# Weight parts made only for the block pairs that use them, and new orders for the second pair and the steady pairs

## The chip, the cores and the metric

One core of one Trainium2 chip. The metric is the device time of one execution in microseconds (us); several runs are taken and the median is compared. The kernel computes in float32; its large products run in a float32 format that TensorE reads in one pass (f32r), each operand split into parts so that the result keeps its precision.

## The reference

A short convolution over time with softmaxed taps per head, then an RMS norm and a SwiGLU feed-forward:

```
x: (8, 4096, 192); weight: (8 heads, 7 taps); d_ff = 1536
w = softmax(weight, axis=-1)
out[b,s,h] = sum_k w[h,k] * x_padded[b, s+k, h]      # 24 channels a head
x = out.reshape(32768, 192)
xn = x / sqrt(mean(x*x) + 1e-6) * rms_g
g = xn @ w_gate;  val = xn @ w_val
return (g * sigmoid(g) * val) @ w_out
```

## The kernel before

**Tiling.** The 32,768 tokens are worked in 32 "pairs" of 2 x 512 tokens. A sequence has 4096 tokens, so every fourth pair begins a new sequence. The 1536 feed-forward columns are 12 blocks of 128, taken as 6 block pairs j = 0..5. For a pair of token halves and a pair of blocks there are four cells a, b, c, d, each holding gate (lower bank) and value (upper bank) in PSUM.

**The two matmul phases of a steady pair.** First the gate and value products: `FORM` says for each j whether the four cells come from 12 direct products (0: words A, B, E for the three thirds of d_model, with the cell's letter) or from 11 (1: words P1 to P7 and Q1 to Q4, a 2x2 scheme over sums of token halves and sums of weight blocks). That makes 3 x 12 + 3 x 11 = 69 products, each of six matmuls (three split parts, two row halves of the array). Then 42 steps o1.k to o7.k, a seven-form 2x2 scheme for the product with w_out; each is six matmuls on 32-column strips and accumulates into one of three PSUM accumulators X, Y, Z. `LINE` is the order of these 111 entries on TensorE.

**Words.** The rest of a pair's work is written as words in `ORDER`, emitted once for each w = 2..32. A word's first letter is the engine (A ScalarE/ACT, V VectorE/DVE, G GpSimd/POOL, S the SyncE DMA queue), then the act; "+" is for the pair after w, "++" two after, "-" the pair before; pN emits N entries of `LINE`. All engines run their own instructions in this order. The acts:

- `gc.j`, `mc.j`: SiLU of a cell's gate (L978) and multiplication with its value (L985); the PSUM bank is free after both. `f1`, `f3`, `f4`, `f5` hand partial sums of the 11-product scheme between banks (L669, L972).
- `h1` to `h4`: the sums of the hidden cells that the seven-form scheme needs (L955). `h2.k` overwrites the cell that form 6 reads.
- `c1`, `s7`, `c2`, `C22`, `C21`, `T11` to `T22`: copies of accumulators, final sums (L1002) and transposes (L943) into the output tile; `st` stores it (L1034). The o3 steps write into X again after C22 has read it.
- For the pair ahead: `ld` loads x (L148; at the start of a sequence `ld.0` issues three transfers instead of one, among them the zeros of L152), `cv0` to `cv6` the taps (L439, L435), `sq`, `red`, `pow`, `bc`, `mul` the norm, `pl` writes the normed tokens to DRAM (L1045), `ft` fetches them back transposed (L640; ft.0 and ft.2 are 512 KB, ft.4 and ft.5 256 KB, ft.1 and ft.3 issue nothing), `x1` to `x4` sums of token halves (L829), and `n`, `l`, `d` with a group number the three split parts (copy or cast L669/L671, subtraction L815, scaled subtraction L817). Groups 0, 1, 2 are the thirds of d_model, 3 and 4 the sums.

**Weight parts.** Ten right-hand operands (o = 0..9), for all 6 block pairs, are made once and kept in DRAM (`wd`). `prepare(o)` makes one in six stages (word `W` runs the next stage): POOL forms the difference (L751), DVE masks off the high bits (L754) and ACT scales a copy (L758), DVE subtracts (L760), POOL subtracts (L764), ACT casts (L766), SP stores (L770). Its buffer alternates between two halves, so operand o waits for the store of o - 2. Operands 2, 4, 6, 8 are used by the 11-product form alone, 9 by the direct form alone; `blocks(o)` says for which j an operand is made. In `FORM = (0, 1, 0, 1, 1, 0)` neither set is evenly spaced, so it returns all six. Steady products read the operands through a ring of ten slots (`ring_load`, L787), each slot refilled when its last product has been issued.

**Start.** Pair 0 is computed without splits. Pair 1, the second pair, runs 24 plain products (`PLAIN`, L873) and its 42 steps in the order `FIRST`, and in its shadow the weight parts are made and pair 2 is normed, placed, fetched and split; word R starts the ring.

## Time and profile before

| | us |
|---|---|
| median of 3 runs (lowest, highest) | 2511.77 (2506.93, 2516.0) |
| the profiled execution's own time | 2515.36 |
| its span, first to last instruction | 2512.7 |
| pair 0, up to the second pair's first product | 125.1 |
| second pair | 125.1 to 233.9 |
| pairs 2 to 31 | 233.9 to 2505.6 |
| after the last matmul | 2505.6 to 2512.7 |

The profile is one execution. In a row of a timeline stand start, duration, engine, source line, operation, what it writes and reads, the number of instructions merged, and in brackets the idle time before it and what ended that. In a row of waits stand the total, how often, and the longest. In a row of a group stand the count, the busy time and mean (ns) of one, and the idle time before them. PE is TensorE's matmuls, PEld its weight loads. Line numbers are those of the kernel before.

### The profile page before, as it was taken

The numbers are of one execution on the slowest core, as the hardware profiler recorded it, in microseconds if no ns is written. First come the engines' busy times: TensorE is split into PE (matmuls) and PEld (weight loads), VectorE is DVE, ScalarE is ACT, GpSimd is POOL, SyncE is SP. The second block draws the span as 40 slices with busy tenths as digits, with TensorE's granted clock in tenths as the row PEclk, the third lists the DMA queues.
The fourth block names the chain that finished last, engine by engine and source line by source line (L and its number), as shares of the span: only waits on it lengthen the run. The fifth ranks groups of instructions, "written<-read, shape, count | busy, mean of one in ns | idle before, by whom it ended". The sixth has DMA issues, their size and how long they took to land.

```text
span 2512.7 us, 69361 instructions
## 1 busy us (share of the span) xinstructions
PE 2468.5 (98%) x29332; PEld 1950.8 (78%) x29332; DVE 2031.6 (81%) x2402; ACT 955.2 (38%) x1344; POOL 1096.0 (44%) x719
## 2 busy tenths in 40 slices
...
GB/s 149 59 215 101 171 198 171 167 169 160 170 200 165 171 152 161 185 184 162 160 163 168 198 168 171 176 166 159 194 175 165 175 162 152 205 164 169 168 151 93
DMA packets 704967, 415.21 MB, mean 165 GB/s; under 512 B 508890, under 2 KB 690962, under 8 KB 704658
## 3 DMA queue, kind: packets, MB, share of 16 engines
...
q14 instruction: 78, 0.64, 0.1%
...
## 4 chain that ended last, share of the span: by engine, by line
PE 90%; DVE 3%; DMA 2%; SPq 2%; issue 1%; POOL 1%; ACT 1%; DVEq 0%; ACTq 0%; POOLq 0%
PE ps L901 56%; PE ps L928 33%; PE ps L873 1%; SPq L148 1%; DVE tt L829 1%; DMA wd<-part 1%; DVE y L439 1%; DMA ht<-in_moe_w_val_dram 0%; DMA ring<-wd 0%; SPq L232 0%; POOL part L764 0%; DVE ht L1100 0%; SPq L1034 0%; DMA hs<-in_moe_w_out_dram 0%; DVE part L760 0%
## 5 line engine op out<-in xcount | busy, mean ns | idle before, releaser
L901 PE MATMUL ps<-part,ring 64*128 64x512 f32 x12420 | 1430.2, 388 | 1.1 <-DVE tt L1002 0.5
L901 PEld LDWEIGHTS ps<-part,ring 64*128 64x128 f32 x12420 | 1196.4, 184 | 228.3 <-issue 13.2
L978 ACT ACTIVATE tt<-ps 128x512 f32<-128x512 f32 x744 | 439.1, 599 | 943.0 <-PE ps L901 859.4
L985 DVE TENSOR_TENSOR ht<-ps,tt 128x512 f32<-128x512 f32 x744 | 498.5, 686 | 292.2 <-ACT tt L978 290.4
L955 POOL TENSOR_TENSOR ht<-ht 128x512 f32<-128x512 f32 x243 | 358.2, 1479 | 459.0 <-PE ps L928 210.3
L928 PE MATMUL ps<-ht,wo_sb 128*32 128x384 f32 (+2 forms) x7272 | 458.4, 383 | 14.3 <-DVE tt L1002 13.4
L928 PEld LDWEIGHTS ps<-ht,wo_sb 128*32 128x32 f32 x7272 | 327.8, 111 | 113.3 <-DVE tt L1002 14.8
L928 PE MATMUL ps<-ht,x 128*32 128x384 f32 (+2 forms) x6696 | 413.2, 379 | 0.0
L439 DVE SCALAR_TENSOR_TENSOR y<-xh,tp,y 128x1536 f32<-128x1536 f32 x186 | 366.8, 1972 | 0.2
L928 PEld LDWEIGHTS ps<-ht,x 128*32 128x32 f32 x6696 | 294.4, 110 | 88.4
L955 POOL TENSOR_TENSOR hs<-ht 128x512 f32<-128x512 f32 x90 | 116.9, 1299 | 427.8 <-DVE ht L985 427.8
L972 DVE TENSOR_TENSOR ps<-ps,tt 128x1024 f32<-128x1024 f32 x180 | 221.9, 1233 | 42.2 <-ACT tt L669 32.9
L955 DVE TENSOR_TENSOR ht<-ht 128x512 f32<-128x512 f32 x129 | 147.0, 1140 | 63.7 <-PE ps L928 63.6
L669 ACT COPY ps<-ps 128x384 f32<-128x384 f32 (+1 forms) x121 | 104.1, 860 | 204.9 <-PE ps L928 147.5
L815 POOL TENSOR_TENSOR part<-xb,part 128x1024 fp32r<-128x1024 f32 x58 | 176.6, 3044 | 0.0
L669 ACT CAST part<-xb 128x1024 fp32r<-128x1024 f32 x87 | 88.6, 1047 | 215.3 <-DMA xb<-xd 214.3
L955 DVE TENSOR_TENSOR ht<-hs,ht 128x512 f32<-128x512 f32 x124 | 165.1, 1351 | 0.3 <-PE ps L928 0.3
L815 POOL TENSOR_TENSOR part<-tt,part 128x1024 fp32r<-128x1024 f32 x30 | 86.2, 2875 | 178.2 <-ACT part L669 178.2
L928 PE MATMUL ps<-hs,x 128*32 128x128 f32 (+2 forms) x2232 | 142.4, 383 | 6.7 <-DVE tt L671 6.7
L817 DVE SCALAR_TENSOR_TENSOR part<-part,xb 128x1024 fp32r<-128x1024 f32 x87 | 131.4, 1511 | 6.9 <-ACT part L669 6.9
L928 PEld LDWEIGHTS ps<-hs,x 128*32 128x32 f32 x2232 | 100.5, 111 | 36.7 <-DVE tt L671 7.0
L669 ACT COPY tt<-ps 128x384 f32<-128x384 f32 (+1 forms) x121 | 106.6, 881 | 21.4 <-PE ps L901 11.3
...
## 6 DMA issues: line engine op xcount, KB each, us to landing
...
xh<-in_x_dram SPq DMA_DIRECT2D x192, 105.0 KB
...
```

The costliest lines, as they stand in the source:

```text
L148: queue(eng).dma_start(out=dst, in_=src)
L439: nc.vector.scalar_tensor_tensor(out=y, in0=xk, scalar=w, in1=y, op0=ALU.mult, op1=ALU.add)
L669: nc.scalar.copy(out=dst, in_=src)
L815: e.tensor_tensor(out=split_of(g, 1).bitcast(F32R), in0=src, in1=high, op=ALU.subtract)
L817: nc.vector.scalar_tensor_tensor(out=split_of(g, 2).bitcast(F32R), in0=high, scalar=1.0 + SPLIT, in1=src, op0=ALU.mult, op1=ALU.subtract,)
L829: engine[eng].tensor_tensor(out=dst, in0=a, in1=b, op=op)
L901: nc.tensor.matmul(out=self.both(j, c)[:, h, :], lhsT=left[HALF[h]], rhs=right[HALF[h]], start=(first and q == 0), stop=True, skip_group_c ...
L928: nc.tensor.matmul(out=self.acc(b)[i * Q : (i + 1) * Q, at : at + n], lhsT=left, rhs=cols, start=fresh, stop=True, skip_group_check=True, ...
L955: engine[eng].tensor_tensor(out=dst, in0=a, in1=b, op=op)
L972: nc.vector.tensor_tensor(out=self.both(j, c), in0=self.both(j, "b"), in1=s5, op=ALU.add)
L978: nc.scalar.activation(out=tt[:, t, :], in_=self.both(j, c)[:, 0, :], func=AF.Silu)
L985: nc.vector.tensor_tensor(out=self.hv(j, "abcd".index(c)), in0=self.both(j, c)[:, 1, :], in1=tt[:, t, :], op=ALU.mult,)
```

## The change

Five things. (1) `HOME` gives each block pair a place in the weights, the three 11-product pairs first (j = 1, 3, 4 in places 0, 1, 2), and all readers of the weights go through it. (2) `blocks(o)` therefore returns three adjacent places for operands 2, 4, 6, 8 and 9, so those five are made and stored with half the columns. (3) `FIRST`, (4) `ORDER` and `LINE` are other orders of the same acts; some acts change engine. (5) Acts for pair 2 that `FIRST` has already done are remembered in `ahead_done` and are not done again when `ORDER` names them for w = 2.

```diff
+    HOME = tuple(
+        sum(FORM[:j]) if on else sum(FORM) + j - sum(FORM[:j]) for j, on in enumerate(FORM)
+    )
     ORDER = (
-        "p2- p6 Vd.3 Vcv3+ p2 Vl.3 VT12- p2 Agd.0 VT21- An.4 p2 Agc.0 Aga.0 Vmc.0 Vmd.0 Gl.4",
-        "p2 Aga.2 Vma.0 Vd.4 Vma.2 Af1.1 Vcv4+ p6 Af3.1 Agb.2 Aga.1 Vf4.1 Vmb.2 p6 Vcv5+",
...
-        "Agd.3 Agc.2 Vmd.3 Agb.3 p3 Vmc.2 Vmb.3 Af1.4 Agd.2 p2 Gh1.1 Gpow+ Vbc+ Gmul+ Af3.4",
-        "Spl.0+ Spl.1+ Vmd.2 Spl.2+ p3 Vf4.4 p1 Spl.3+ Spl.4+ Spl.5+ p4 Spl.6+ Spl.7+ Aga.4",
-        "Sst1.1- Sld.0++ Sst0.4- Vma.4 Sft.0+ Sft.1+ Sft.2+ Sst1.3- Sst0.3- Sft.4+ Vf5.4",
-        "Sft.3+ Sld.1++ Sst0.0- Agb.5 Agc.4 Sld.2++ Sst0.2- p1 Sld.3++ Sst1.2- Sld.4++",
-        "Sld.5++ Sld.6++ Sft.5+ p2 Vh1.3 Vmb.5 Agd.4 Agb.4 p3 Vmd.4 Sld.7++ Sst0.1- Sst1.0-",
-        "Vmb.4 p2 Agc.5 p4 Vh1.4 Vmc.4 Gh3.1 Gh1.2 Gh3.2 Gh3.0 Agd.5 Aga.5 Vmd.5 Vh1.5 Vma.5",
-        "p6 Gh3.4 Vh3.3 Vh2.0 Vh2.4 Vmc.5 p2 Vh2.2 Ac1 An.0+ Vd.0+ Vx3+ Vh2.3 Gh3.5 p7 An.1+",
-        "As7 Gh2.1 Gh2.5 p6 An.2+ p4 Vh4.4 Gh4.2 Gx1+ Gl.0+ Vc2 p7 Gh4.0 p2 Gh4.3 p2 Vh4.5",
-        "Vd.1+ Vh4.1 Vx2+ Vl.2+ Vd.2+ An.3+ Acv0++ Vx4+ Gl.1+ VC22 VT11 Vcv1++ VT22 p2 VC21",
-        "p2 Vcv2++",
+        "p4 Vd.2 p1 Vd.3 Vcv1+ VT12- p4 Vcv2+ p2 Vcv3+ p1 Agd.0 Aga.2 An.4 Aga.0 Gl.4 Vmd.0",
+        "Vma.2 Vma.0 p4 Sst1.4- Agc.0 Vmc.0 Vcv4+ Af1.1 p1 Af3.1 Vf4.1 p1 Vd.4 p2 Agb.2 p1",
...
+        "Vred+ Agd.3 Agc.2 Vmd.3 p1 Vmc.2 Vmc.3 p4 Agb.3 Gh1.0 Gh1.1 Gpow+ Vmb.3 Af1.4 p3",
+        "Agd.2 Vbc+ Vh3.0 Gmul+ Af3.4 Vmd.2 Spl.0+ p2 Spl.1+ Spl.2+ Spl.3+ Spl.4+ Vf4.4 p5",
+        "Sst0.0- Spl.5+ Spl.6+ Sst0.4- Aga.4 Gh1.3 Vh1.2 Vma.4 Vf5.4 Vh3.1 Spl.7+ Agb.5 Agc.4",
+        "Sld.0++ p3 Agd.4 Vh3.2 Vmb.5 Vmc.4 p1 Vmd.4 Sft.2+ Sft.0+ Sft.1+ Sst1.1- Sst1.2-",
+        "Sst0.1- Sft.3+ Sft.4+ p7 Agb.4 Agc.5 p1 Aga.5 Vmb.4 Vma.5 p4 Sft.5+ Sld.1++ p3 Vmc.5",
+        "Agd.5 Vmd.5 Vh2.0 Gh3.3 Gh1.4 Vc1 Gh3.4 An.0+ Gh1.5 Gh2.4 Gh2.3 Gh2.1 Vh3.5 Vh2.2",
+        "Vx1+ Vx2+ Vh2.5 p15 As7 Gh4.4 Ac2 p9 An.1+ An.2+ Sld.2++ Sld.3++ Sst1.0- Sst0.2-",
+        "Sld.4++ Sst0.3- Sst1.3- Sld.5++ Gh4.3 Gh4.1 Gx3+ Sld.6++ Sld.7++ Acv0++ Vh4.0 Vh4.2",
+        "Vx4+ Vn.3+ Vd.0+ Vl.0+ Vl.3+ Vh4.5 VC22 p4 Gl.2+ p6 Vd.1+ VT22 Vl.1+ VC21 p1 VT11",
+        "VT21",
     )
     FIRST = (
-        "p1 Vcv5+ W p2 Vcv6+ p1 Aga.0 Vma.0 p2 Asq+ W W p1 Agb.0 W Vmb.0 W p1 Vred+ p2 Agc.0",
...
-        "Gh2.5 p1 Vh2.2 p1 Gh2.1 Sld.3++ p1 Ac1 Vh2.3 An.0+ p2 Sld.4++ An.1+ Vd.0+ p1 Sld.5++",
-        "p1 As7 p1 Sld.6++ Vx3+ p1 Gh4.2 p2 Gx1+ p1 Sld.7++ p1 Vd.1+ Gl.0+ Gl.1+ An.2+ Vd.2+",
-        "Vl.2+ Vx2+ Vx4+ R p2 Vh4.4 p1 Gh4.0 p1 Vh4.5 p1 Vc2 p2 Vh4.1 p4 An.3+ p1 Acv0++ p2",
-        "VC22 p1 VT11 Gh4.3 p1 Vcv1++ p2 VC21 p3 Vcv2++ VT22",
+        "p1 W p3 Aga.0 Vma.0 p2 W W p1 Agb.0 W Vmb.0 W p3 Agc.0 Vmc.0 W p1 W Vcv5+ W W p1 W",
...
+        "p1 Gh2.1 p1 Vc1 Vh2.5 Vx1+ p2 Vx2+ Sld.1++ p1 Gh4.1 p1 Vh4.0 Sld.2++ p1 Vh4.2",
+        "Sld.3++ p2 Vx4+ p1 Vn.3+ p1 Vd.0+ Sld.4++ p1 Vl.0+ p2 As7 An.1+ Vd.1+ Vl.1+ An.2+",
+        "Vd.2+ Gl.2+ Gx3+ R Vl.3+ p1 Sld.5++ Gh4.4 p1 Sld.6++ p2 Ac2 Sld.7++ p2 Vh4.5 p4 VT11",
+        "Gh4.3 p3 Acv0++ VC22 p6 VC21 p4 VT22 VT21",
     )
     LINE = (
-        "Aa.0 Ad.0 Ed.0 Bd.0 Ac.0 Ec.0 Ea.0 Bc.0 Ba.0 Aa.2 Ea.2 Ba.2 Ab.2 P1.1 Bb.2 P5.1 P6.1",
...
-        "Ea.5 o1.0 o1.4 o7.0 o7.2 o1.5 o1.2 o1.1 o1.3 o7.4 o7.1 o7.5 o7.3 o6.4 o2.2 o6.2 o6.5",
-        "o6.0 o4.4 o6.1 o2.4 o2.0 o2.5 o6.3 o4.1 o2.1 o5.1 o5.3 o5.4 o5.2 o4.5 o5.5 o5.0 o2.3",
-        "o4.0 o4.2 o4.3 o3.5 o3.3 o3.1 o3.4 o3.2 o3.0",
+        "Aa.2 Ba.2 Ad.0 Aa.0 Bd.0 Ac.0 Ea.2 Ed.0 Ec.0 Ea.0 Ba.0 Bc.0 P1.1 Ab.2 P5.1 Bb.2 P6.1",
...
+        "Ed.5 o1.0 o1.4 o1.2 o1.3 o1.1 o1.5 o7.0 o7.4 o2.1 o2.0 o2.2 o7.3 o6.2 o6.0 o7.5 o6.1",
+        "o7.2 o7.1 o2.4 o6.5 o6.4 o6.3 o4.2 o2.5 o5.1 o5.0 o5.5 o2.3 o5.2 o5.3 o5.4 o4.4 o4.0",
+        "o3.2 o4.3 o4.5 o4.1 o3.4 o3.3 o3.5 o3.0 o3.1",
     )
@@ blocks
-        mine = [j for j in range(NP) if kind in (None, FORM[j])]
-        step = {b - a for a, b in zip(mine, mine[1:])}
-        if len(step) > 1:
-            return slice(0, NP)
-        return slice(mine[0], mine[-1] + 1, step.pop() if step else 1)
+        mine = sorted(HOME[j] for j in range(NP) if kind in (None, FORM[j]))
+        return slice(mine[0], mine[-1] + 1)
@@ ring_load
-        r = (j * NW + o) * P
+        r = (HOME[j] * NW + o) * P
@@ products (the plain ones)
-                                out=self.both(j, c)[:, h, :], lhsT=wf[HALF[h], k, 2 * j + f, :],
+                                out=self.both(j, c)[:, h, :], lhsT=wf[HALF[h], k, 2 * HOME[j] + f, :],
@@ step
-            right = RIGHT[form][:, k]
+            right = RIGHT[form][:, HOME[k]]
@@ run
+    ahead_done = set()
...
-                    if own_acts[act] <= p < PAIRS:
+                    if own_acts[act] <= p < PAIRS and (name, p) not in ahead_done:
                         ahead(eng, name, p)
+                        if w == 1:
+                            ahead_done.add((name, p))
```

28 rows, old and new, of tables (FIRST, LINE, ORDER) are left out of this document.

## Prediction, made before the changed kernel ran

> **What bounds the kernel now.** I read the page first, then TensorE's waits, then its busy time stretch by stretch.
>
> ```profile
> span 2512.7 us, 69361 instructions
> ...
> PE 2468.5 (98%) x29332; PEld 1950.8 (78%) x29332; DVE 2031.6 (81%) x2402; ACT 955.2 (38%) x1344; POOL 1096.0 (44%) x719
> ...
> L901 PE MATMUL ps<-part,ring 64*128 64x512 f32 x12420 | 1430.2, 388 | 1.1 <-DVE tt L1002 0.5
> ```
> ```profile
> PE ps L928 <- DVE tt L1002: 13.4, 5, 4.1
> PE ps L873 <- DVE ht L985: 7.2, 6, 2.2
> PE ps L928 <- DVE tt L671: 6.7, 1, 6.7
> ```
> ```profile
> 125.11:197.68 72.57, 65.36 (x290) 28.26 (x288) 50.54 (x61) 28.98 (x44) 32.62 (x19) 0.98 0.71 211
> 197.68:233.91 36.23, 29.52 (x506) 22.05 (x504) 28.85 (x27) 6.92 (x8) 16.35 (x8) 0.91 0.24 60
> 233.91:2505.64 2271.73, 2257.24 (x27542) 1828.79 (x27540) 1856.26 (x2141) 854.03 (x1163) 1013.25 (x652) 1.00 0.65 169
> 2280.80:2430.70 149.90, 149.90 (x1840) 121.40 (x1838) 124.95 (x145) 55.94 (x77) 67.56 (x44) 1.00 0.62 168
> 534.40:610.90 76.50, 75.23 (x922) 60.14 (x920) 62.68 (x73) 28.78 (x39) 33.69 (x22) 1.00 0.66 170
> 836.30:916.70 80.40, 76.62 (x920) 63.82 (x918) 66.42 (x74) 28.66 (x39) 33.59 (x22) 0.98 0.64 162
> 1142.05:1222.70 80.65, 76.83 (x920) 62.18 (x918) 66.70 (x74) 28.65 (x39) 33.69 (x22) 0.98 0.62 161
> 1748.00:1824.20 76.20, 75.19 (x920) 59.63 (x920) 63.15 (x73) 28.66 (x39) 33.34 (x22) 1.00 0.66 171
> 2049.80:2130.80 81.00, 76.93 (x922) 60.96 (x920) 66.73 (x74) 28.66 (x39) 33.89 (x22) 0.98 0.63 160
> ```
>
> TensorE is the bound, and the matmul count does not change. The columns are length, then busy time of PE, PEld, DVE, ACT, POOL, the granted clock, the DMA share. The fourth row is two clean pairs without a gap: 74.95 us a pair. Thirty pairs would take 2248.5; they take 2271.7 (third row), 23.2 more. The last five rows, single pairs, hold 394.75 - 5 x 74.95 = 20.0 of that. These are pairs in which the first load of a new sequence is issued (there are 32/4 sequences; seven such loads fall into this stretch). So three places can give time: those five pairs (20.0), the second pair (first two rows) and the end.
>
> **The five late pairs.** Rows of the SP queue, of ACT and of DVE, from the pair at 1066.85 (clean) and the one at 1142.05 (late):
>
> ```profile
> 1126.25 0.70 SPq L640 DMA_DIRECT2D xb<-xd  x1
> ...
> 1187.40 0.74 SPq L152 DMA_DIRECT2D xh<-x  x1
> ...
> 1204.01 0.71 SPq L640 DMA_DIRECT2D xb<-xd  x1
> ```
> ```profile
> 1120.44 1.99 ACT L669 CAST part<-xb 128x1024 fp32r<-128x1024 f32 x2
> ...
> 1129.75 1.05 ACT L669 CAST part<-xb 128x1024 fp32r<-128x1024 f32 x1 [6.62 <-DMA xb<-xd]
> ...
> 1197.72 1.05 ACT L669 CAST part<-xb 128x1024 fp32r<-128x1024 f32 x1 [1.26 <-DMA xb<-xd]
> ...
> 1209.20 1.04 ACT L669 CAST part<-xb 128x1024 fp32r<-128x1024 f32 x1 [10.06 <-DMA xb<-xd]
> ```
> ```profile
> 1136.08 0.68 DVE L829 TENSOR_TENSOR tt<-xb,tt 128x512 f32<-128x512 f32 x1
> ...
> 1210.28 1.23 DVE L815 TENSOR_TENSOR part<-xb,part 128x1024 fp32r<-128x1024 f32 x1 [1.43 <-ACT part L669]
> 1211.42 2.31 DVE L817 SCALAR_TENSOR_TENSOR part<-part,xb 128x1024 fp32r<-128x1024 f32 x1
> 1213.65 2.82 DVE L829 TENSOR_TENSOR tt<-xb,tt 128x512 f32<-128x512 f32 x1
> ```
> ```profile
> 1113.46:1126.25 12.79, 12.79 (x230) 9.66 (x230) 10.91 (x11) 4.05 (x6) 6.90 (x5) 1.00 0.97 204
> ```
>
> The last fetch of the next pair's tokens is issued 59.4 us into the clean pair and 62.0 into the late one (the sequence's zeros and its extra first rows stand ahead of it); its data are used at 62.9 and 67.2, 4.3 us apart. Between the first fetch and the last, the DMA engines are at 0.97: the queue is full, so the order of issues is what counts. Behind this fetch stand An.2, then Vl.2 and Vd.2 on DVE, then Vx4 beside POOL's work (2.82 for 0.68), then C22 (L1002), for which TensorE waits up to 4.1.
>
> The new order takes Vl.2 off DVE (POOL does it, Gl.2, behind C22 in the words) and puts Vd.2 into the next pair. The first product that reads token group 2 is now Ea.2, the seventh in the line, where it was Ed.0, the third. One product is 1430.2 / 2070 = 0.69 us, so Ea.2 is due at 74.95 + 6 x 0.69 = 79.1. The cast (1.05) and POOL's subtraction (3.0, row below) must fit before that, so a landing up to about 75 harms nobody; 67.2 was harmful before. It also issues the last fetch ahead of seven loads instead of behind most of them. I take 17 of the 20.0; at most 20, at least 8 if the first fetches become late instead (rivals).
>
> A cheaper stall also saves clock: the 80 to 81 us pairs show 0.98 granted, the 76 us ones 1.00. The Trainium skill (TensorE: Matmul & The Clock Gate, the section on what is actually happening) says that an idle window of about 3.4 us halves the clock; the trace agrees, with 1.00 beside the 76.50 pair and 0.98 beside the 80.65 one. By that rule alone, cutting a 4.1 us gap to under 3.4 would also give back the roughly 1.5 us that these pairs lose beyond the gap.
>
> **Work that changes engine.** Per pair, the built order has one split subtraction fewer on POOL, one copy fewer on ACT (An.3 becomes Vn.3) and both on DVE; Gx1, Vx3 become Vx1, Gx3, and c1, c2 swap engines.
>
> ```profile
> L815 POOL TENSOR_TENSOR part<-xb,part 128x1024 fp32r<-128x1024 f32 x58 | 176.6, 3044 | 0.0
> ...
> L669 ACT CAST part<-tt 128x1024 fp32r<-128x1024 f32 x59 | 61.6, 1044 | 73.3 <-DVE tt L829 73.3
> ...
> L815 DVE TENSOR_TENSOR part<-xb,part 128x1024 fp32r<-128x1024 f32 x29 | 35.2, 1214 | 5.7 <-ACT part L669 5.7
> ```
>
> DVE gains 1.2 (the subtraction) and a 128x1024 copy that no row shows: 0.6 (half of 1.2) to 1.2. I take 0.8, so 2.0 a pair on 62.5 of 74.95: it stays under TensorE. Does it lie ahead of C22? Before it stand as many splits (Vn.3, Vd.0, Vl.0, Vl.3 for Vd.0, Vd.1, Vl.2, Vd.2) and x sums (three) as before; the rest follows C22, where two taps (1.97 each) have left for the next pair's start. C22 is due earlier: the first o3 step is the 34th of 42 instead of the 37th, 3 x 0.65 = 2.0 us (a step is (74.95 - 69 x 0.69) / 42 = 0.65). No row says that every pair meets this. I take nothing for it, between -1 (nothing hidden remains to be won: the clean pair has no gap) and +9 us (0.3 in each of 30).
>
> **The second pair.**
>
> ```profile
> 125.11 26.02 PE L873 MATMUL ps<-xb,part 64*128 64x512 f32 x120
> ```
> ```profile
> L764 POOL TENSOR_TENSOR part<-part 128x768 f32<-128x768 f32 x10 | 19.3, 1930 | 36.2 <-DVE part L760 36.2
> ...
> L760 DVE SCALAR_TENSOR_TENSOR part<-part 128x768 f32<-128x768 f32 x10 | 9.9, 988 | 5.4 <-ACT part L758 5.0
> ...
> L754 DVE TENSOR_SCALAR part<-part 128x768 uint32<-128x768 uint32 x10 | 7.4, 736 | 8.3 <-DMA wd<-part 8.2
> ```
> ```profile
> 212.44 2.86 DVE L829 TENSOR_TENSOR tt<-tt,ring 128x512 f32<-128x512 f32 x1
> ...
> 220.25 0.54 DVE L671 COPY tt<-ps 128x384 f32<-128x384 f32 x1
> ```
>
> Ten products without a gap take 26.02, so 24 take 62.4; the first row of the stretches has 72.57: 10.1 lost. TensorE waits there for L985, which queues on DVE behind the making of weight parts. DVE stands 8.2 for the store of the part two before (same half of the buffer) and 5.0 for ACT's copy. Five of ten parts shrink from 768 to 384 columns. By the mean durations that saves at most 5 x (0.99 + 0.74) / 2 = 4.3 us on DVE, 5 x 1.93 / 2 = 4.8 on POOL, and half of five stores; 3 of the 8 store waits are then for a half part. I take 6 of the 10.1; bounds 2 and 9.
>
> Its 42 steps, 27.3 at 0.65 each, took 36.23: 8.9 lost, 6.7 of it waiting for Vc2, which stood on DVE behind x sums and splits slowed beside POOL. Ac2 now stands on ACT. But C22 still stands behind all of DVE's splits and is due at step 34, and T11 must free its bank for the third pair. I take 4 of the 8.9 back; bounds -1 and 7.
>
> **The end.**
>
> ```profile
> 2506.17 4.17 ACTq L1034 DMA_DIRECT2D out_dram<-o_sb  x6
> ```
>
> After the last matmul (2505.6) ACT issues six stores in 4.17 us, 0.70 each. Now VT21 stands ahead of VT12 and three of ACT's six are issued while TensorE still works: at most 2.1 less, at least 0.5 (one store hidden); I take 1.8.
>
> **The sum.** 17 + 0 + 6 + 4 + 1.8 = 28.8, less 1 that I allow for new small waits: 28. The profiled execution took 2515.4 (span 2512.7 and 2.7 around it), 3.6 over the median of 2511.77, so it becomes 2487.4, and the median 2484. Bounds by the terms: 20+1+9+7+2 = 39 (2473) and 8-9+2-1+0.5 = 0.5 (2511).
>
> **Rivals.** (1) The first fetches become the late ones, in every pair: slower. x1 on DVE needs both 512 KB fetches, Vx1, Vx2, Vh2.5 stand in a row, and h2.5 is read by o6.5, the 20th step, due at 69 x 0.69 + 19 x 0.65 = 60.0. The three last 0.7 each, or up to 2.8 beside POOL: x1 must start by about 57. In the late pair the second fetch landed 55.65 in (1197.72). Now three ring loads of 192 KB stand ahead where one 96 KB store stood: 480 KB more, 2.4 us at 204 GB/s. That makes 58 in late pairs, at worst 54.6 + 2.4 = 57 in clean ones (there the second of the two casts at 1120.44 ran without a wait, from about 1121.4). So it decides from about 57: for the seven late pairs 1 us each is in my 17; if clean pairs miss it by 2 us, 30 x 2 = 60 less the 28 gives 2511.8 + 32 = 2544, by 1.2 us it gives 2520. Against it: in the clean pair no wait for the two first fetches shows, only one for the last.
>
> (2) DVE, with 2.0 us more, reaches C22 late in every pair: by 1 us, 2511.8 - 28 + 30 = 2514. For it: Vx4 took 2.82 beside POOL. The Trainium skill (SBUF — State Buffer, Terms) says that VectorE and GpSimd hold a shared port pair by an exclusive lock, so the loser fully blocks; the trace agrees with 2.82 against 0.68. By that rule an unlucky order could add a whole POOL instruction, 3.04 us, in each pair: an estimate of 91 us. Against it: POOL has one such instruction less, and Vl.2 no longer follows the late fetch.
>
> (3) The late pairs remain, since the zeros still stand ahead of the fetches, and only the second pair and the end gain: 2511.8 - 11.8 = 2500.
>
> (4) The parts are made as before, because their stores, not their length, set the pace: second pair gains nothing, 2484 + 10 = 2494.
>
> **How the numbers follow.** Forecast 0.55 (its own range 2474 to 2496), (4) 0.12, (3) 0.13, (1) 0.10, (2) 0.10. Range 2473 to 2513: it takes in (3), (4), the bounds and part of (2). This kernel's measurement tells 0.3%, 7.5 us, from no change. So faster ends at 2504 and slower begins at 2519. Faster: the forecast, (4) and all but 0.02 of (3), 0.78; slower: 0.09 of (1) and 0.04 of (2), 0.13; same: the rest, 0.09.
>
> **What would show it.** Right: no pair over 76 us in the third stretch, no wait of TensorE for L1002 of 4 us, products of the second pair in under 68 us, ACT's last cast waiting without anybody behind it, three stores of ACT after the last matmul. Wrong: a clean pair over 75.3, DVE idle before L829 for xb's fetch, TensorE waiting for L1002 or L943 in every pair.

## The result and the profile after

| | before | after |
|---|---|---|
| median of 13 runs each (lowest, highest), us | 2513.41 (2502.91, 2519.47) | 2497.24 (2493.61, 2505.38) |
| ratio of the times, 95% interval | | 0.9947 (0.9932, 0.9961) |
| the profiled execution's time, its span | 2515.36, 2512.7 | 2502.22, 2498.5 |
| second pair begins at | 125.1 | 124.3 |
| its 24 products | 72.57 | 62.74 |
| its 42 steps | 36.23 | 36.77 |
| pairs 2 to 31 | 2271.7 | 2269.6 |
| from the last matmul to the end | 7.04 | 5.09 |

The change made the kernel faster by 0.5%, 14.2 us by the spans and 16.2 by the medians; 28 had been forecast. The time is inside the range, and about half of the forecast gain is there. Line numbers from here on are those of the changed kernel: up to the making of the weight parts they are three higher (L442 for L439, L672 for L669, L674 for L671), from L750 on the same; e8, below, has the numbers of the kernel before.

The same stretches, with the same columns as in the prediction (length, busy time of PE, PEld, DVE, ACT, POOL, granted clock, DMA share, GB/s); the last row is one pair:

```profile
124.33:187.07 62.74, 62.27 (x291) 27.71 (x289) 43.80 (x61) 25.87 (x44) 24.52 (x19) 1.00 0.61 189
187.07:223.83 36.76, 31.00 (x506) 23.21 (x504) 28.94 (x29) 4.39 (x6) 15.27 (x8) 0.91 0.32 73
223.83:2493.43 2269.60, 2257.34 (x27544) 1840.96 (x27540) 1829.75 (x2199) 830.98 (x1135) 1025.92 (x623) 1.00 0.66 169
602.20:679.20 77.00, 75.28 (x922) 62.77 (x920) 63.12 (x79) 28.99 (x39) 36.70 (x21) 1.00 0.67 169
```

The products of the second pair lost their gaps (62.27 busy of 62.74). The steps and the thirty steady pairs did not get shorter. Yet no steady pair is as late as the three of 80 to 81 us of before: five take over 76 us, and the longest are the one in the last row and the one at 830.49, 77.0 each. What took the place of the late pairs is in TensorE's waits (total, times, longest):

```profile
PE ps L901 <- DVE o_sb L943: 11.4, 16, 1.7
PE ps L928 <- DVE tt L1002: 3.5, 1, 3.5
PE ps L928 <- DVE ps L674: 2.3, 1, 2.3
```

Before, the largest row was C22 (L1002), 13.4 us in five waits. Now it is a transpose, L943, in many small ones. The two others are both in the second pair's steps. This is the start of the 77.0 us pair in the timeline, first TensorE, then DVE:

```profile
602.18 3.69 PE L901 MATMUL ps<-part,ring 64*128 64x512 f32 x30
607.60 4.60 PE L901 MATMUL ps<-part,ring 64*128 64x512 f32 x38 [1.73 <-DVE o_sb L943]
```
```profile
597.61 0.64 DVE L943 STREAM_TRANSPOSE o_sb<-tt 128x256 f32<-128x256 f32 x2 [0.70 <-issue]
598.17 3.30 DVE L815 TENSOR_TENSOR part<-xb,part 128x1024 fp32r<-128x1024 f32 x1
...
604.05 1.21 DVE L817 SCALAR_TENSOR_TENSOR part<-part,tt 128x1024 fp32r<-128x1024 f32 x1
605.18 1.81 DVE L442 SCALAR_TENSOR_TENSOR y<-xh,tp,y 128x1536 f32<-128x1536 f32 x1
606.91 0.63 DVE L943 STREAM_TRANSPOSE o_sb<-ps 128x256 f32<-128x256 f32 x2
```

Thirty matmuls are five products. The sixth, Ac.0, writes into the bank that still holds the accumulator of the pair before, and is free once VT12 (L943) has read it. VT12 ends at 607.54, and TensorE goes on at 607.60. In the words of the new `ORDER`, "p4 Vd.2 p1 Vd.3 Vcv1+ VT12-", a tap of 1.81 us (L442) and two subtractions stand on DVE ahead of it. In a clean pair VT12 ends 3.7 us after the pair's start, the wait is some 0.2 us, and the pair takes 75.3; here VT12 ends 5.4 us in, and TensorE lost 1.7. Over the thirty pairs, by the start times of the matmuls, the entry ahead of Ac.0 takes 16.9 us more than thirty products without a gap.

The fetches no longer hold TensorE up, though ACT waits for transfers in every pair (its rows of waits). DVE's taps, which follow ACT's (L438), stood idle for it only 2.1 us in the whole run:

```profile
ACT part L672 <- DMA xb<-xd: 233.2, 31, 9.5
ACT y L438 <- DMA xh<-in_x_dram: 225.3, 28, 17.6
```

And at the end the stores begin 1.7 us ahead of the last matmul's end (2493.43), where they began 0.5 behind it:

```profile
2491.70 4.31 ACTq L1034 DMA_DIRECT2D out_dram<-o_sb  x6
```

### The profile page after: what moved, and what is told of

It is laid out like the page before. It is cut to its first block, busy times and chain, and to the rows that moved or that the text cites. A ratio compares the mean times of both kernels' runs of the same rounds, so it can differ in the third digit from the quotient of the medians.

```text
span 2498.5 us, 69292 instructions
## 1 busy us (share of the span) xinstructions
PE 2466.9 (99%) x29332; PEld 1963.2 (79%) x29332; DVE 1998.1 (80%) x2461; ACT 926.4 (37%) x1314; POOL 1099.6 (44%) x690
## 4 chain that ended last, share of the span: by engine, by line
PE 65%; DVE 12%; SPq 10%; DMA 9%; issue 2%; POOL 1%; ACT 0%; DVEq 0%; POOLq 0%; ACTq 0%
PE ps L901 53%; PE ps L928 10%; DMA xb<-xd 6%; SPq L151 5%; DVE part L817 3%; SPq L1034 3%; DVE y L442 2%; DVE o_sb L943 2%; PE ps L873 2%; DVE part L815 1%; DMA xh<-in_x_dram 1%; DMA out_dram<-o_sb 1%; SPq L643 1%; SPq L787 1%; DVE ht L955 1%
## 5 line engine op out<-in xcount | busy, mean ns | idle before, releaser
L901 PE MATMUL ps<-part,ring 64*128 64x512 f32 x12420 | 1436.2, 389 | 12.3 <-DVE o_sb L943 11.4
L901 PEld LDWEIGHTS ps<-part,ring 64*128 64x128 f32 x12420 | 1212.2, 184 | 229.6 <-DVE o_sb L943 24.5
L985 DVE TENSOR_TENSOR ht<-ps,tt 128x512 f32<-128x512 f32 x744 | 486.4, 686 | 243.3 <-ACT tt L978 239.1
L955 POOL TENSOR_TENSOR hs<-ht 128x512 f32<-128x512 f32 x150 | 247.3, 1657 | 592.8 <-DVE ht L985 592.8
L928 PE MATMUL ps<-ht,wo_sb 128*32 128x384 f32 (+2 forms) x7272 | 458.5, 381 | 6.6 <-DVE tt L1002 3.5
L928 PEld LDWEIGHTS ps<-ht,wo_sb 128*32 128x32 f32 x7272 | 331.2, 110 | 102.2 <-issue 15.4
L928 PE MATMUL ps<-ht,x 128*32 128x256 f32 (+2 forms) x6696 | 407.6, 380 | 0.0
L928 PEld LDWEIGHTS ps<-ht,x 128*32 128x32 f32 x6696 | 290.8, 110 | 90.0 <-issue 0.7
L955 POOL TENSOR_TENSOR ht<-ht 128x512 f32<-128x512 f32 x153 | 258.4, 1697 | 231.8 <-PE ps L928 227.1
L442 DVE SCALAR_TENSOR_TENSOR y<-xh,tp,y 128x1536 f32<-128x1536 f32 x186 | 350.6, 1885 | 3.2 <-ACT y L438 2.1
L815 POOL TENSOR_TENSOR part<-tt,part 128x1024 fp32r<-128x1024 f32 x30 | 72.2, 2407 | 286.5 <-ACT part L672 286.5
L672 ACT CAST part<-xb 128x1024 fp32r<-128x1024 f32 x87 | 90.3, 1049 | 249.4 <-DMA xb<-xd 233.2
L672 ACT COPY tt<-ps 128x1024 f32<-128x1024 f32 (+1 forms) x152 | 121.8, 801 | 156.7 <-PE ps L928 147.4
L955 POOL TENSOR_TENSOR ht<-hs,ht 128x512 f32<-128x512 f32 x93 | 144.8, 1583 | 9.2 <-PE ps L928 9.2
L928 PE MATMUL ps<-hs,x 128*32 128x128 f32 (+2 forms) x2232 | 140.1, 379 | 0.0
L438 ACT ACTIVATE y<-xh,tp 128x1536 f32<-128x1536 f32 x29 | 45.8, 1580 | 233.0 <-DMA xh<-in_x_dram 225.3
L928 PEld LDWEIGHTS ps<-hs,x 128*32 128x32 f32 x2232 | 98.6, 110 | 30.0
L672 ACT COPY ps<-ps 128x1024 f32<-128x1024 f32 x90 | 89.7, 997 | 71.4 <-PE ps L901 64.1
```

The costliest lines, as they stand in the source:

```text
L442: nc.vector.scalar_tensor_tensor(out=y, in0=xk, scalar=w, in1=y, op0=ALU.mult, op1=ALU.add)
L672: nc.scalar.copy(out=dst, in_=src)
L815: e.tensor_tensor(out=split_of(g, 1).bitcast(F32R), in0=src, in1=high, op=ALU.subtract)
L901: nc.tensor.matmul(out=self.both(j, c)[:, h, :], lhsT=left[HALF[h]], rhs=right[HALF[h]], start=(first and q == 0), stop=True, skip_group_c ...
L928: nc.tensor.matmul(out=self.acc(b)[i * Q : (i + 1) * Q, at : at + n], lhsT=left, rhs=cols, start=fresh, stop=True, skip_group_check=True, ...
L955: engine[eng].tensor_tensor(out=dst, in0=a, in1=b, op=op)
```

## Experiments

Twelve kernels ran, in four groups (e1, e3, e4 and e5; e6 to e8; e9 to e11; e12 and e13), each beside the kernel before. That had medians of 2511.27, 2522.25, 2525.09 and 2523.07 there, so ratios of different groups are not compared closer than half a per cent; stages come from the profiled execution of each.

| kernel | median, us | ratio to before | 24 products | 42 steps | 30 pairs | end | span |
|---|---|---|---|---|---|---|---|
| before | | | 72.57 | 36.23 | 2271.7 | 7.04 | 2512.7 |
| after | 2497.24 | 0.9947 (0.9932, 0.9961) | 62.74 | 36.77 | 2269.6 | 5.09 | 2498.5 |
| e1 | 2489.27 | 0.991 (0.9887, 0.9933) | 62.73 | 36.44 | 2254.1 | 5.37 | 2482.9 |
| e3 | 2499.81 | 0.995 (0.9927, 0.9973) | 64.77 | 36.35 | 2273.3 | 7.01 | 2505.8 |
| e4 | 2505.50 | 0.9982 (0.9963, 1.0001) | 67.67 | 36.71 | 2266.5 | 5.11 | 2500.4 |
| e5 | 2492.97 | 0.9925 (0.99, 0.9949) | 72.45 | 36.46 | 2250.7 | 7.04 | 2491.0 |
| e6 | 2492.09 | 0.9889 (0.9856, 0.9921) | 62.75 | 28.57 | 2273.0 | 5.03 | 2494.2 |
| e7 | 2486.60 | 0.9867 (0.9833, 0.9901) | 64.47 | 36.96 | 2250.1 | 7.06 | 2483.3 |
| e8 | 2598.31 | 1.0315 (1.0279, 1.0351) | 72.53 | 36.42 | 2364.2 | 7.03 | 2605.6 |
| e9 | 2484.34 | 0.9832 (0.9804, 0.9861) | 62.75 | 28.56 | 2266.0 | 5.09 | 2486.8 |
| e10 | 2490.84 | 0.986 (0.9835, 0.9886) | 62.75 | 34.92 | 2267.2 | 5.26 | 2494.5 |
| e11 | 2514.81 | 0.9965 (0.9947, 0.9983) | 62.75 | 36.24 | 2284.2 | 5.11 | 2512.4 |
| e12 | 2479.95 | 0.9832 (0.981, 0.9854) | 65.22 | 28.94 | 2250.5 | 7.07 | 2476.1 |
| e13 | 2481.68 | 0.984 (0.9816, 0.9865) | 65.19 | 28.95 | 2250.6 | 5.01 | 2474.2 |

### e1: the transposes ahead of the tap (e1_t12_before_tap)

The changed kernel with two words exchanged in `ORDER`.

```diff
-        "p4 Vd.2 p1 Vd.3 Vcv1+ VT12- p4 Vcv2+ p2 Vcv3+ p1 Agd.0 Aga.2 An.4 Aga.0 Gl.4 Vmd.0",
+        "p4 Vd.2 p1 Vd.3 VT12- Vcv1+ p4 Vcv2+ p2 Vcv3+ p1 Agd.0 Aga.2 An.4 Aga.0 Gl.4 Vmd.0",
```

> The changed kernel with one word moved: VT12- (the transpose that frees accumulator X's bank) stands ahead of the tap Vcv1+ instead of behind it. Theory A (the steady pairs lose at Ac.0, the first product that needs the fourth PSUM bank, because that bank is freed by T12, which DVE reaches behind two splits and a tap): T12 ends about 1.7 us earlier (one tap, 1.80 less the transpose's own place), the entry before Ac.0 falls from a median of 1.11 us to 0.68, the excess there from 16.9 us over 30 pairs to under 3, and the kernel becomes 12 to 17 us shorter, ratio to before about 0.988. Rival B (the tap put back makes the following DVE work late, the wait moves to another product): ratio 0.993 to 0.996, with a wait of TensorE for L985 or L972 instead. Rival C (the loss is in the order of the products itself, not a wait): no change at that entry, ratio 0.9947.

The thirty pairs fell by 15.5 us. The row of L943 in TensorE's waits fell from 11.4 us in 16 waits to 0.2 in one; this is the largest that stands there for products (L901) now, and the same place on DVE as above:

```profile
PE ps L901 <- DVE ht L985: 1.8, 3, 0.9
```
```profile
599.43 1.21 DVE L817 SCALAR_TENSOR_TENSOR part<-part,tt 128x1024 fp32r<-128x1024 f32 x1
600.57 0.64 DVE L943 STREAM_TRANSPOSE o_sb<-ps 128x256 f32<-128x256 f32 x2
601.13 5.48 DVE L442 SCALAR_TENSOR_TENSOR y<-xh,tp,y 128x1536 f32<-128x1536 f32 x3
606.52 2.52 DVE L985 TENSOR_TENSOR ht<-ps,tt 128x512 f32<-128x512 f32 x4
```

By the profiled executions the order of two words on DVE held back all of the 13.8 us that were missing from the forecast. That is the upper end: the profiled execution of e1 is the fastest of its runs (2484.66), that of the changed kernel one of the slowest of its own (2502.22). By the medians, 2489.27 against 2497.24, it is 8 us, of different groups; against e4 (below), which ran beside it with the changed kernel's order, it is 16.2 less the 4.9 that e4's products take longer, 11.3 us. The last two rows show why this order stays tight: the three taps now stand right ahead of the multiplications of the cells (L985), which free the next banks.

### e3 and e4: the halved parts alone, and the new orders without them (e3_home_alone, e4_all_blocks)

e3 is the kernel before with `HOME`, its readers and the new `blocks`, in the old orders. e4 is the changed kernel in which `blocks` returns all six places:

```diff
-        return slice(mine[0], mine[-1] + 1)
+        return slice(0, NP)
```

> The kernel before with the weights' places, the five half-width parts and nothing else: FIRST, ORDER and LINE as before. Theory (DVE's work and the store waits of the parts make the plain products late): the second pair's 24 products, 72.6 us before, fall to 66 to 69, its 42 steps stay at 36.2, the steady pairs keep their five late ones; kernel 3 to 6 us shorter, ratio 0.9975 to 0.999. Rival (the stores set the pace whatever their width, or the waits only shift): products within 1 us of 72.6, ratio 1.000.

> The changed kernel with every weight part made for all six block pairs, in the new orders. Theory (half of the second pair's gain is the halved parts, half the new FIRST): its 24 products, 62.2 us in the changed kernel, become 66 to 69, the rest unchanged, kernel 4 to 7 us longer than the changed one, ratio about 0.997. Rival (the new FIRST alone does it, the halving is hidden): products within 1 us of 62.2, ratio 0.9947.

The products of the second pair: 72.57 before, 64.77 with the halving alone (7.8 less, where 66 to 69 us had been expected), 67.67 with the new orders alone (4.9 less), 62.74 with both (9.8 less). Halving is most of it, and the two overlap, since TensorE is busy for 62.3 of the last. In e3 the late pairs are still there (30 pairs 2273.3, three of them at 82): halving does nothing for the steady state.

### e5: one word of the fetch (e5_last_fetch_early)

The kernel before with `Sft.5+` taken from behind `Sld.6++` and put right behind `Sft.4+`.

```diff
-        "Sst1.1- Sld.0++ Sst0.4- Vma.4 Sft.0+ Sft.1+ Sft.2+ Sst1.3- Sst0.3- Sft.4+ Vf5.4",
+        "Sst1.1- Sld.0++ Sst0.4- Vma.4 Sft.0+ Sft.1+ Sft.2+ Sst1.3- Sst0.3- Sft.4+ Sft.5+ Vf5.4",
...
-        "Sld.5++ Sld.6++ Sft.5+ p2 Vh1.3 Vmb.5 Agd.4 Agb.4 p3 Vmd.4 Sld.7++ Sst0.1- Sst1.0-",
+        "Sld.5++ Sld.6++ p2 Vh1.3 Vmb.5 Agd.4 Agb.4 p3 Vmd.4 Sld.7++ Sst0.1- Sst1.0-",
```

> The kernel before with one word moved: Sft.5+ (the last fetch of the next pair's tokens) stands right behind Sft.4+, ahead of the seven later loads, instead of behind them. Theory (the five late pairs come from this fetch's place in the DMA queue): its landing is 8 us earlier, no pair over 76 us remains, TensorE's wait for L1002, 13.4 us in all, goes to under 2, kernel 15 to 20 us shorter, ratio 0.992 to 0.994. Rival (only moving its consumers off the path helps, or the late pairs are made by the two extra loads' own DMA time): the late pairs stay at 80 us, ratio 0.999 to 1.001. Rival two (the loads, now behind the fetch, make the first tap late): TensorE waits for a tap's followers in every pair, ratio over 1.000.

All thirty pairs take 74.9 to 75.4, 2250.71 in all, with TensorE busy for all but 0.2 us of it:

```profile
233.29:2484.00 2250.71, 2250.50 (x27542) 1813.00 (x27540) 1848.09 (x2141) 852.50 (x1163) 1019.13 (x652) 1.00 0.66 171
```

The place of that one fetch on SP's queue was the cause of the five late pairs, and it can be cured without a new order.

### e6, e10, e9: the second pair's steps (e6_steps_order, e10_loads_alone, e9_loads_before_ring)

All three are e1 with other words in `FIRST`. e6 moves two words; e10 moves R behind the third pair's last input loads instead; e9 does both.

```diff
 e6 and e9:
-        "p1 Gh2.1 p1 Vc1 Vh2.5 Vx1+ p2 Vx2+ Sld.1++ p1 Gh4.1 p1 Vh4.0 Sld.2++ p1 Vh4.2",
+        "p1 Gh2.1 p1 Ac1 Vh2.5 Vx1+ p2 Vx2+ Sld.1++ p1 Gh4.1 p1 Vh4.0 Sld.2++ p1 Vh4.2",
 e6:
-        "Vd.2+ Gl.2+ Gx3+ R Vl.3+ p1 Sld.5++ Gh4.4 p1 Sld.6++ p2 Ac2 Sld.7++ p2 Vh4.5 p4 VT11",
-        "Gh4.3 p3 Acv0++ VC22 p6 VC21 p4 VT22 VT21",
+        "Vd.2+ Gl.2+ Gx3+ R p1 Sld.5++ Gh4.4 p1 Sld.6++ p2 Ac2 Sld.7++ p2 Vh4.5 p4 VT11",
+        "Gh4.3 p3 Acv0++ VC22 Vl.3+ p6 VC21 p4 VT22 VT21",
 e10:
-        "Vd.2+ Gl.2+ Gx3+ R Vl.3+ p1 Sld.5++ Gh4.4 p1 Sld.6++ p2 Ac2 Sld.7++ p2 Vh4.5 p4 VT11",
+        "Vd.2+ Gl.2+ Gx3+ Vl.3+ p1 Sld.5++ Gh4.4 p1 Sld.6++ p2 Ac2 Sld.7++ R p2 Vh4.5 p4 VT11",
```

> The changed kernel with VT12- ahead of Vcv1+ in the steady order (as in e1_t12_before_tap) and, in the second pair's order alone, two words moved: the h update's add Vc1 goes from DVE to ACT (Ac1), and Vl.3+ goes from right behind R to right behind VC22. Theory: the second pair's 42 steps cost 36.4 us in place of a forecast 32 because DVE's queue ahead of Vc1 and of C22's sums is too long (waits of 2.3 and 3.5 us at those two places in the changed kernel). Then the steps take 30 to 33 us, and the span is 3 to 6 us below e1_t12_before_tap's 2482.9, ratio to before about 0.989. Rival: what the steps wait for is the loads and DVE's work as a whole, not the place of two words; then the wait moves to T11 or another word, the steps stay at 36 to 37 us and the span at 2482 to 2484.

> e1_t12_before_tap with R alone moved behind the last three input loads in the second pair's order (Ac1 and Vl.3+ as in the changed kernel). Theory: in e1_t12_before_tap the late input is hidden, since the steps end late anyway: Acv0 no longer waits until 221, but the steps stay at 36 to 37 us, the third pair at 75, and the span at 2481 to 2484, no gain. Rival: the steps' own waits (Vc1, C22) or those of pairs 3 to 17 come from the late input; then the span falls below 2478.

> e6_steps_order with one word more moved in the second pair's order: R, the loads of the weight ring, which SP cannot issue before POOL has read the last tokens out of that ring (210.86 us in e6_steps_order), goes from ahead of the last three loads of the next pair's input (Sld.5++ to Sld.7++) to behind them. Theory: in e6_steps_order the steps took 28.6 us, but the third pair 87.2, because its input stood behind R on SP, its first tap Acv0 waited for it until 223.4, and DVE's taps and sums behind Acv0 came late (TensorE waited 8.5 us). With the input ahead of R the steps stay at 28 to 30 us, the third pair falls to 75 to 77, the thirty pairs take 2254 to 2260, and the span is 2475 to 2481, ratio to before 0.983 to 0.988. Rival: the third pair is late because of DVE's and POOL's work as a whole, or the ring comes too late; then the third pair stays over 82 us and the span at 2488 or more.

In e6 the steps fell to 28.6, even below what was expected, and the next pair gave back more than that (87.2 for 75). Stretches (the steps, then the third pair), SP's queue, ACT, TensorE:

```profile
187.53:216.10 28.57, 27.86 (x506) 20.64 (x505) 22.90 (x28) 4.85 (x7) 17.89 (x8) 1.00 0.23 52
216.10:303.30 87.20, 78.01 (x924) 65.65 (x920) 61.80 (x73) 29.27 (x39) 35.60 (x21) 0.94 0.65 163
```
```profile
210.86 4.60 SPq L787 DMA_DIRECT2D ring<-wd  x10
215.58 5.15 SPq L151 DMA_DIRECT2D xh<-in_x_dram  x3
```
```profile
223.35 1.58 ACT L438 ACTIVATE y<-xh,tp 128x1536 f32<-128x1536 f32 x1 [20.79 <-DMA ring<-wd]
```
```profile
233.10 12.08 PE L901 MATMUL ps<-part,ring 64*128 64x512 f32 x80 [8.54 <-DVE ht L985]
```

R cannot be issued before POOL has read the last tokens out of the ring (210.8), and the third pair's last input loads stand behind R. So the tap Acv0, which needs this input (the profile names the ring's transfers, issued just ahead on the same queue), comes at 223.4, its successors on DVE later, the multiplications (L985) behind those later still, and TensorE waits 8.5 us. With R behind the loads (e9) that pair takes 74.92 us:

```profile
215.68:290.60 74.92, 74.92 (x924) 59.48 (x920) 60.03 (x73) 27.12 (x38) 32.96 (x21) 1.00 0.72 185
```

e10 shows that moving R alone brings only 1.5 us in the steps (34.9). The theory held for the steps and the third pair; what it missed is the sum, 2486.8 in place of 2475 to 2481, because the thirty pairs show 2266.0. In e10 they show 2267.2 with the same steady order that took 2254.1 in e1. Most of the added time is in pairs of 76 to 79 us all along the run, where TensorE waits for the multiplications behind the three taps of e1, or for h sums of the steps. One such pair of e10, on DVE:

```profile
444.84 0.64 DVE L943 STREAM_TRANSPOSE o_sb<-tt 128x256 f32<-128x256 f32 x2 [0.73 <-DMA out_dram<-o_sb]
445.40 3.28 DVE L815 TENSOR_TENSOR part<-xb,part 128x1024 fp32r<-128x1024 f32 x1
...
452.38 0.64 DVE L943 STREAM_TRANSPOSE o_sb<-ps 128x256 f32<-128x256 f32 x2
452.94 5.48 DVE L442 SCALAR_TENSOR_TENSOR y<-xh,tp,y 128x1536 f32<-128x1536 f32 x3
```

This pair starts at 449.38. The subtraction at 445.40 took 3.28, as in the 77.0 us pair of the changed kernel, and VT12 ended 3.6 us into the pair where it ended 2.0 into that of e1 (599.23). So e1 moved the first victim of a late DVE out of the way, not the lateness itself.

Where the lateness of such pairs begins can be read in the first row: ahead of VT22 (L943), DVE stood idle for 0.73 until a store of the output tile was done. VT22 writes into one of two output buffers (`outs`), which the stores of the pair before must have left, and these stand on SP among the input loads. Of the seven pairs of e10 over 76.4 us, the first waits for an h sum; in the six others DVE stood idle for 0.7 to 3.1 ahead of VT22, and in no other pair for more than 0.3. In the changed kernel the two 77.0 us pairs have 0.70 and 0.82 there, and no other has more than 0.4. This is the sum over the whole run of e10:

```profile
L943 DVE STREAM_TRANSPOSE o_sb<-tt 128x256 f32<-128x256 f32 x62 | 25.9, 419 | 10.2 <-DMA xh<-in_x_dram 4.7 <-DMA out_dram<-o_sb 4.3 <-issue 1.1
```

The last column is the idle time: 10.2 in e10, 4.1 in e9, 3.5 in e1, 1.9 in the changed kernel, and 0.0 in the old order (e12). The profile puts a part down to input loads (xh), which VT22 does not read. No run moves these stores, so this is read from the traces and not tested. Why the stores come late in some pairs and executions and not in others stays open, as does the smaller lateness of pairs between 75.4 and 76.3.

### e8: the consumer moved in place of the fetch (e8_consumer_later)

```diff
-        "Vd.1+ Vh4.1 Vx2+ Vl.2+ Vd.2+ An.3+ Acv0++ Vx4+ Gl.1+ VC22 VT11 Vcv1++ VT22 p2 VC21",
+        "Vd.1+ Vh4.1 Vx2+ An.3+ Acv0++ Vx4+ Gl.1+ VC22 VT11 Vl.2+ Vd.2+ Vcv1++ VT22 p2 VC21",
```

> The kernel before with the fetch left where it is, and its consumers on DVE moved instead: Vl.2+ Vd.2+ go from ahead of VC22 to behind VT11. Theory: the late pairs come from DVE standing at Vl.2, which waits for the last fetch, while C22's sums stand behind it; with nothing behind it that TensorE needs soon, the five pairs of 76 to 81 us fall to 75 to 76, the 30 pairs take 2250 to 2256 us, and the ratio is 0.992 to 0.994. Rival: what makes the pairs late is the fetch itself, needed by the same date wherever its consumer stands; then the wait goes on to the transposes or to the second difference's products and the 30 pairs stay at 2265 us or more, ratio 0.998 to 1.002.

Both were wrong: 29 of 30 pairs became late, by 3 to 6 us.

```profile
PE ps L901 <- DVE tt L1002: 76.7, 29, 2.7
```
```profile
1017.21 1.84 DVE L815 TENSOR_TENSOR part<-xb,part 128x1024 fp32r<-128x1024 f32 x1
1018.97 3.40 DVE L817 SCALAR_TENSOR_TENSOR part<-part,xb 128x1024 fp32r<-128x1024 f32 x1
1022.29 1.80 DVE L439 SCALAR_TENSOR_TENSOR y<-xh,tp,y 128x1536 f32<-128x1536 f32 x1
1024.02 0.62 DVE L943 STREAM_TRANSPOSE o_sb<-tt 128x256 f32<-128x256 f32 x2
1024.57 0.51 DVE L1002 TENSOR_TENSOR tt<-ps,tt 128x384 f32<-128x384 f32 x1
```

The wait for C22 (TensorE's L928 on L1002) is indeed gone, but the two splits now stand between C22 and C21, and C21 frees the bank of the next pair's first product. The two splits took 5.24 there, and TensorE waits 2.6 us in nearly every pair. The rest of the lateness is clock: TensorE is busy for 2287 us of the thirty pairs at a granted clock of 0.98, where it was 2257 at 1.00. DVE has no such time to spare between the two.

### e11: the fetch put back (e11_fetch_late)

e1 with `Sft.5+` moved from ahead of `Sld.1++` to behind `Sld.7++`; its users stay where the change put them.

```diff
-        "Sst0.1- Sft.3+ Sft.4+ p7 Agb.4 Agc.5 p1 Aga.5 Vmb.4 Vma.5 p4 Sft.5+ Sld.1++ p3 Vmc.5",
+        "Sst0.1- Sft.3+ Sft.4+ p7 Agb.4 Agc.5 p1 Aga.5 Vmb.4 Vma.5 p4 Sld.1++ p3 Vmc.5",
...
-        "Sld.4++ Sst0.3- Sst1.3- Sld.5++ Gh4.3 Gh4.1 Gx3+ Sld.6++ Sld.7++ Acv0++ Vh4.0 Vh4.2",
+        "Sld.4++ Sst0.3- Sst1.3- Sld.5++ Gh4.3 Gh4.1 Gx3+ Sld.6++ Sld.7++ Sft.5+ Acv0++ Vh4.0 Vh4.2",
```

> e1_t12_before_tap with the last fetch, Sft.5+, put back behind the seven loads in the steady order (from ahead of Sld.1++ to behind Sld.7++), about where the kernel before had it; its consumers stay where the change put them (An.2 on ACT, Gl.2 on POOL, Vd.2 in the next pair). Theory of the prediction: the consumers' new places alone would do, as the tokens are first read by the seventh product of the next pair; the late pairs stay away, the thirty pairs take 2254 to 2258 us and the ratio is 0.990 to 0.993. Rival: the place of the fetch is needed too, since An.2 stands on ACT ahead of Acv0 and the steps' last copies, and Gl.2 comes late for Ea.2; then some pairs of new sequences go over 76 us and the thirty pairs take 2262 us or more, ratio 0.994 or above.

The rival held: 2284.2 for the thirty pairs, 13 of them over 76. The pair that starts at 602.50:

```profile
602.80 1.23 DVE L817 SCALAR_TENSOR_TENSOR part<-part,xb 128x1024 fp32r<-128x1024 f32 x1 [1.66 <-DMA xb<-xd]
603.95 3.42 DVE L817 SCALAR_TENSOR_TENSOR part<-part,tt 128x1024 fp32r<-128x1024 f32 x1
607.29 0.63 DVE L943 STREAM_TRANSPOSE o_sb<-ps 128x256 f32<-128x256 f32 x2
```

Vd.2 stands at the front of the pair on DVE and waits for the fetch, and T12 stands behind it. The second subtraction then runs beside POOL's Gl.2, released by the same fetch at 602.84 (3.45 us), and takes 3.42. T12 ends 5.4 us into the pair, as late as in the changed kernel's 77.0 us pair, though the product that reads those tokens would have had time.

### e7, e12, e13: the old orders with few words moved (e7_halved_and_fetch, e12_copy_on_act, e13_t21_in_own_pair)

e7 is e3 and e5 together. e12 is e7 with the copy Vc2 of the second pair on ACT. e13 is e12 with VT21 in its own pair, in `ORDER` and `FIRST`.

```diff
 e12 and e13, FIRST:
-        "Vl.2+ Vx2+ Vx4+ R p2 Vh4.4 p1 Gh4.0 p1 Vh4.5 p1 Vc2 p2 Vh4.1 p4 An.3+ p1 Acv0++ p2",
+        "Vl.2+ Vx2+ Vx4+ R p2 Vh4.4 p1 Gh4.0 p1 Vh4.5 p1 Ac2 p2 Vh4.1 p4 An.3+ p1 Acv0++ p2",
 e13, ORDER (the same in FIRST):
-        "p2- p6 Vd.3 Vcv3+ p2 Vl.3 VT12- p2 Agd.0 VT21- An.4 p2 Agc.0 Aga.0 Vmc.0 Vmd.0 Gl.4",
+        "p2- p6 Vd.3 Vcv3+ p2 Vl.3 VT12- p2 Agd.0 An.4 p2 Agc.0 Aga.0 Vmc.0 Vmd.0 Gl.4",
...
-        "Vd.1+ Vh4.1 Vx2+ Vl.2+ Vd.2+ An.3+ Acv0++ Vx4+ Gl.1+ VC22 VT11 Vcv1++ VT22 p2 VC21",
+        "Vd.1+ Vh4.1 Vx2+ Vl.2+ Vd.2+ An.3+ Acv0++ Vx4+ Gl.1+ VC22 VT11 Vcv1++ VT22 p2 VC21 VT21",
```

> The kernel before with two things alone: the weight parts halved by the blocks' new places (as in e3_home_alone) and the one word Sft.5+ moved ahead in the steady order (as in e5_last_fetch_early); both old orders otherwise. Theory: the two gains are independent and add: start 124.4, the second pair's products 64.8, its steps 36.4, the 30 pairs 2250.7, the end 7.0, so a span of 2483.3 and a ratio of about 0.989 to before, the same as e1_t12_before_tap. Then the whole second search of the orders is worth no more than one moved word. Rival: the halved parts shift the stores of the second pair into the first steady pairs, or the late pairs come back with them; then the 30 pairs take 2258 us or more and the ratio is 0.992 or above.

> e7_halved_and_fetch (both old orders, halved parts, the fetch moved ahead) with one word more: the second pair's second copy Vc2 goes from DVE, where it stood behind x sums and splits and made TensorE wait 6.7 us, to ACT (Ac2), whose queue is empty then. In this old order all of the third pair's input is issued ahead of R, and its first tap was done at 209.4 us. Theory: the 6.7 us go down to some 2.5 us, which h4.5 on DVE (ends at 210.7) still costs; the steps take 30 to 33 us in place of 37.0, the thirty pairs stay at 2249 to 2253, and the span is 2477 to 2481, ratio to before 0.983 to 0.986. Rival: as in e6_steps_order, what the steps gain is lost in the third pair and behind it; then the thirty pairs take 2256 us or more and the span stays at 2482 to 2487.

> e12_copy_on_act with VT21 moved from the next pair's start (VT21-, behind VT12-) to right behind VC21 in its own pair, in both orders, so that in the last pair half of the output is stored while TensorE still works, as in the changed kernel. Theory: the end falls from 7.0 to about 5.1 us and nothing else moves: the span is 1.5 to 2 us below e12_copy_on_act's. Rival: the transposes (0.6 us) behind C21 hold up the taps and sums behind them on DVE; then the thirty pairs grow by 0.3 us or more each, 9 us or more in all, and the kernel is slower than e12_copy_on_act.

e7's span is 2483.3, as the sum of the stages of e3 and e5 gave: the two gains are independent. e12's steps fell from 36.96 to 28.94, below the 30 to 33 expected, and nothing was given back behind them, as here the input loads have always stood ahead of R:

```profile
124.38:189.60 65.22, 62.55 (x291) 28.50 (x289) 43.47 (x61) 25.77 (x44) 25.00 (x19) 1.00 0.67 191
189.60:218.54 28.94, 27.64 (x506) 20.80 (x504) 27.82 (x23) 7.40 (x9) 16.61 (x8) 1.00 0.24 72
218.54:2469.04 2250.50, 2250.38 (x27544) 1824.84 (x27540) 1849.26 (x2144) 853.07 (x1163) 1017.86 (x652) 1.00 0.67 171
```
```profile
204.80 0.48 ACT L672 COPY tt<-ps 128x384 f32<-128x384 f32 x1 [5.72 <-PE ps L928]
```

e13's end is 2.06 us shorter and its thirty pairs are the same; the medians of e12 and e13 do not tell them apart. Both beat both kernels: the slowest of their nine runs, 2485.69, lies under the fastest of the changed kernel's thirteen, 2493.61. With the halved parts, one fetch, one copy (and one transpose) moved, the old orders run 1.6 to 1.7% faster than before.

## Why the prediction was wrong, point by point

| term of the sum | forecast | measured (spans) |
|---|---|---|
| late pairs | 17 | 20.0 |
| work that changes engine | 0 (bounds -1 to +9 of loss) | -16.9 |
| second pair's products | 6 (2 to 9) | 9.8 |
| second pair's steps | 4 (-1 to 7) | -0.5 |
| end | 1.8 | 2.0 |
| other small waits of the thirty pairs | -1 | -1.0 |

With 0.8 that came before the second pair, the last column makes the 14.2.

**The step that failed** is the one on work that changes engine: "I take nothing for it", where it cost 16.9 us. It was not DVE's load: with 58 instructions more, DVE's busy time over the thirty pairs fell from 1856.26 to 1829.75, where 2.0 more a pair had been expected. The step looked at one deadline on DVE, C22, and at what stands ahead of it. C22 was indeed not late: TensorE's wait of 3.5 us for L1002 is the second pair's, and the steady pairs show none of this kind. The same paragraph says that two taps "have left for the next pair's start"; what it left out is that VT12, which frees a bank for the sixth product, stands right behind the first of them. Vd.2, Vd.3, a tap and the transposes are 1.21 + 1.21 + 1.81 + 0.63 = 4.9 us without any slowing, and that product is due 3.5 us into the pair (five products at 0.69), so DVE had to be done with the pair before 1.4 us ahead of the pair's start. In the clean pair that starts at 375.76 it begins Vd.2 1.6 us ahead, and Vd.2 takes 1.86 there; in the 77.0 us pair it begins 0.8 us behind. This was in the order and could have been added up. Its place was named only as a sign of failure ("TensorE waiting for L1002 or L943 in every pair") and given no price. e1 shows the cause by undoing it: no pair of it is held up by more than 0.4 us at that product.

Rival (2) had the mechanism, DVE late in every pair, with the wrong victim. Its rule can now be checked. The Trainium skill (SBUF — State Buffer, Terms) says that the pair of ports is held for a whole instruction and the loser blocks. In the 77.0 us pair POOL's subtraction ran ahead of DVE's (3.30), in the clean pair that starts at 375.76 it began behind DVE's (1.75):

```profile
598.02 2.37 POOL L815 TENSOR_TENSOR part<-xb,part 128x1024 fp32r<-128x1024 f32 x1
```
```profile
371.58 3.38 POOL L815 TENSOR_TENSOR part<-xb,part 128x1024 fp32r<-128x1024 f32 x1
```
```profile
370.95 1.75 DVE L815 TENSOR_TENSOR part<-xb,part 128x1024 fp32r<-128x1024 f32 x1
```

The rest of POOL's instruction at 598.17 is 2.22, and with DVE's own 1.21 that gives 3.43; measured is 3.30, so the trace agrees. In the clean pair it is POOL that takes 1.0 more. So a DVE that is 0.8 late (0.70 of it the idle time at 597.61, for which that row names no cause) meets POOL in the other order and is 2.3 late behind it. In the other 77.0 us pair, at 830.49, the row of the same instruction names the store of the output tile:

```profile
826.08 0.64 DVE L943 STREAM_TRANSPOSE o_sb<-tt 128x256 f32<-128x256 f32 x2 [0.82 <-DMA out_dram<-o_sb]
```

The forecast took 1.21 for the subtraction that came to DVE; its group costs 88.2 us for 58 where 29 cost 35.2, 1.8 each for the added ones. The copy, forecast 0.8, has a median of 0.68 and a mean of 0.90:

```profile
L815 DVE TENSOR_TENSOR part<-xb,part 128x1024 fp32r<-128x1024 f32 x58 | 88.2, 1520 | 0.0
...
L674 DVE CAST part<-tt 128x1024 fp32r<-128x1024 f32 x30 | 27.0, 901 | 0.0
```

**The late pairs**: the wait for C22 went in all five; one of them, at 830.49, is late again, now by the wait for VT12. The reason given was half right. "A landing up to about 75 harms nobody", because the first product that reads the tokens is due at 79.1, is refuted by e11: a fetch is due when the first instruction that waits for it stands ahead of something urgent, and here that is Vd.2 with T12 behind. What cured the pairs is the fetch's place on SP (e5).

**The second pair's products** gained beyond the upper bound. The bound counted the halving alone and held for it (7.8 in e3); the new order took 2 us more. Rival (4), that the stores set the pace, falls with e3.

**The steps** gained nothing: the wait of 6.7 for Vc2 went, and waits of 2.3 (Vc1) and 3.5 (C22) came, both on DVE's queue. The prediction names C22 there, with no price but the lower bound of -1. The rest is clock: TensorE is busy for 31.00 us of these steps at 0.91 and for 27.64 at 1.00 in e12, 3.4 us beyond the waits themselves. In the changed kernel the granted clock is 0.50 in two stretches of 3.41 us that begin within 0.8 us of the ends of the waits of 2.3 and 3.5, and half of the two is the 3.4:

```profile
195.52:198.93 3.41, 3.41 (x40) 2.46 (x34) 3.37 (x5) 0.00 (x0) 1.27 (x1) 0.50 0.00 0
216.00:219.41 3.41, 3.03 (x30) 2.10 (x34) 0.33 (x1) 0.00 (x0) 0.00 (x0) 0.50 1.01 326
```

The Trainium skill (TensorE: Matmul & The Clock Gate, What's actually happening) has an idle window of about 3.4 us halve the clock. The trace agrees on the half and on the length, but here a wait of 2.3 was enough; in e10 the same wait of 2.3 left the clock at 1.00.

**The end** was right in place and size.
